# Attention and two dense layers on one core: weight conversions spread over slots 5 to 25, layer 1's last piece behind attention's last product, kept PSUM banks, and two last output transfers

## The chip, the core and the metric

One Trainium2 chip, of which the kernel uses one core. The metric is the device time of one execution in microseconds (us). The engines named below are TensorE (PE, with its weight loads as PEld), VectorE (DVE), ScalarE (ACT), GpSimd (POOL) and SyncE (SP), which here issues nearly every DMA.

## The reference, cut to what matters

Block-causal attention for 4 batches, 8 heads, 576 positions and head size 64, then two dense layers over all 2304 tokens (512 to 2048 to 512), the first with a leaky gate, the second with an exponential one.

```python
scores = scale * np.matmul(q, k.transpose(0, 1, 3, 2))
scores = np.where(block_i >= block_j, scores, -1e9)     # blocks of 64 positions
attn = softmax(scores)                                  # float32
x = np.matmul(attn, v)                                  # -> 2304 x 512
h = x @ w_in;  g = np.maximum(h, 0.0) + alpha * np.minimum(h, 0.0)
x = g @ w_out                                           # layer 1
h = x @ w2_in; g = np.where(h > 0.0, h, np.exp(np.minimum(h, 0.0)) - 1.0)
out = g @ w2_out                                        # layer 2
```

The weights arrive as 64-bit numbers. The kernel turns each into a high and a low 32-bit part, and most products are made in three passes over such parts.

## The kernel before

**Two stages.** The first is attention, as 71 *slots* (k = 0 to 70) written out by hand in `slot`; the second is both dense layers, as a list of steps behind it. Every engine executes its instructions in the order in which the program emits them. The tokens lie in five units: 0 to 3 have 512 tokens each, and unit 4 has 256, the last 64 positions of every batch (the "tails").

**Slots.** Slots 0 to 7 and 32 to 39 make the scores of the first 256 positions of a pair of heads, slots 8 to 31 and 40 to 63 those of the rest, three slots for a pair; slots 64 to 70 finish. In a slot PE makes scores (L290, L297, L302), the products of an earlier pair with v (L444) and transposes of an earlier slot's exponentials (L377, L384, L390); DVE takes maxima (L319), sums (L353, L355), low parts of x (L89) and copies of transposes (L95); ACT makes the exponentials (L346) and copies; POOL normalises (L96) and makes low parts. The product of the last pair (L444 in slot 70) gives the last piece of `x1[3]` and of the tails, which DVE finishes with two low parts (L89, outputs x and xtail).

**Weights.** `load_w` handles half of one of 16 weight tiles per layer. The DMA (L123) is issued at a slot in `w_slots`, `arrival[0]` ticks later ACT makes two conversions (L133, L134) and DVE three operations behind them (L138, L139, L143), here called the *begin*; then POOL adds (L148), ACT casts (L162) and DVE makes the low part (L89, output w), the *end*. A tick is one slot, or two pieces of layer 1. Sixteen halves are loaded beside attention: the first eight serve hidden tiles 0 to 3, the other eight hidden tiles 4 to 7.

**Layer 1 beside attention.** Three units (0, 2 and 1) go partly through layer 1 beside attention, in `l1_beside`, with the first 4 of 16 hidden tiles. Each is cut into 16 *pieces* of 6 products of 512 columns: 8 for the hidden tiles (L599) and 8 for the outputs (L611). `stretches` says from which slot to which the pieces are spread. For unit 0 the hidden pieces stand from slot 14 to 26 and the output pieces from 26 to 39: ahead of slots 26, 28, 29, 31, 33, 34, 36 and 37. The last 8 pieces of unit 1 stand one ahead of each of slots 63 to 70.

**Banks.** In attention PSUM is four banks for scores (`twin`) and banks 4 to 7, used in turn for transposes, products and layer 1's pieces (`ring("t", ...)`). Behind attention `att.close()` gives up all eight, and a new pool takes them; the dense stage uses banks 5, 6, 7 for hidden tiles (`ring("h", ...)`) and 0 to 4 for sums (`ring("acc", ...)`). Its first step is unit 3 (hidden tiles L580, outputs L684), straight from `x1[3]` in SBUF; unit 4 is next and is read back from scratch (`load_x1`, L542).

**Scratch.** Units are dumped to scratch from SP, two ticks behind the product that completes them: L424 for a unit, L426 for the tails.

**The end.** The last unit of layer 2 is unit 4, with two blocks of 128 tokens. Each block's last sum is copied from PSUM to SBUF (DVE for block 0, ACT for block 1), and then L670 writes it in two transfers of 64 rows of 2 KB. Whole blocks of other units go out at L666, one transfer of 128 rows each.

Of the kernel before, what the change touches and what calls it, by code (L numbers as in the profile page):

```python
# [9 lines left out]
F32 = mybir.dt.float32  # L10
# [6 lines left out]
PSUM = bass.MemoryType.PSUM  # L17
DRAM = bass.MemoryType.DRAM

P = 128  # L20
B, H, S, D = 4, 8, 576, 64
# [15 lines left out]
def f32(ap):  # L37
    return ap.bitcast(F32)
# [3 lines left out]
def attention_moe_kernel(ctx: ExitStack, tc: tile.TileContext, qT, kT, v_a, v_b, w1, w2, alpha, out):  # L42
    nc = tc.nc
    pe, act, dve, pool_e = nc.tensor, nc.scalar, nc.vector, nc.gpsimd
# [21 lines left out]
    rings = {}  # L66

    def ring(name, *banks):
        rings[name] = list(banks)
# [33 lines left out]
    def later(ticks, emit):  # L103
        due.setdefault(tick[0] + ticks, []).append(emit)
# [83 lines left out]


    att = ExitStack()  # L190
    ps = att.enter_context(pool("ps", 1, space=PSUM))
    twin = [ps.tile([P, 2, 512], F32, name=f"pair{i}") for i in range(2)]
    bank = [None] * 4 + [ps.tile([P, 512], F32, name=f"bank{i}") for i in range(4, 8)]
    ap1 = att.enter_context(pool("att1", 1))
    ap2 = att.enter_context(pool("att2", 2))
    vraws = [ap1.tile([P, 2, 5, D], F32, name=f"vraw{i}") for i in range(2)]
# [222 lines left out]
    def x_out(n, half):  # L419

        b, p = PAIRS[n]
        u = unit_of(n, half)
        if n % (2 * NPAIR) == 2 * NPAIR - 1:
            later(2, lambda: nc.sync.dma_start(out=xd[u], in_=f32(x1[u])))  # L424
        if half == 1:
            later(2, lambda: nc.sync.dma_start(out=xd[B][:, :, p, 64 * b:64 * b + 64], in_=f32(st[n]["tail"])))  # L426

# [227 lines left out]
    def l2_y(u, f, gs):  # L655
        for tg in range(UNITS[u] // P):
            acc = acc_bank(tg, f == 0)
            for t, (wp_, gp_) in enumerate(PASSES):
                pe.matmul(acc, gs[:, gp_, tg * P:(tg + 1) * P], w_out(1, f, wp_, 0, DM),  # L659
                          start=f == 0 and t == 0, stop=f == NF - 1 and t == 2)  # L660
            if f == NF - 1:
                o = z_tile(tg)
                copy("va"[tg % 2], o, acc)
                if u < B:
                    r = S * (2 * (u % 2) + tg // 2) + 256 * (u // 2) + P * (tg % 2)
                    nc.sync.dma_start(out=out[r:r + P, :], in_=o)  # L666
                else:
                    for k in range(2):
                        r = S * (2 * tg + k) + 512
                        nc.sync.dma_start(out=out[r:r + 64, :], in_=o[64 * k:64 * k + 64, :])  # L670


    zs = {}
# [24 lines left out]
    with tc.manual_schedule(engines={ET.PE, ET.Activation, ET.DVE, ET.Pool, ET.SP}):  # L698
        ring("s", 0, 1)
        ring("t", 4, 5, 6, 7)  # L700

        halves = [(0, f, r) for r in range(2) for f in range(FA)]
        load_early(0)
        load_early(1)
        keep_busy(6)
        for half in range(2):
            scale_early(0, slice(256 * half, 256 * half + 256), "v")
        load_early_v(0)
        load_alpha()
        for emit in other_at[-1]:  # L710
            emit()
        load_early_v(1)
        end_tick()
        LEAD = 14
        stretches = [(0, LEAD, 26, 26, X_DONE[2]), (2, X_DONE[2], 47, 47, 55), (1, 55, 63, 63, LAST)]
        w_slots = {5, 8, 10, 12, 14, 16, 18, 20}
        w_slots |= {27 + 5 * i for i in range(8)}
        halves += [(0, FA + f, r) for r in range(2) for f in range(4)]

        def slots(lo, hi):  # L720
            for k in range(lo, hi):
                if k in w_slots:
                    arrival[0] = 4 if k > 21 else 3 if k < 8 else 2
                    load_w(*halves.pop(0))
                slot(k)

        slots(0, LEAD)

        k = LEAD
        for u, a, b, c, d in stretches:  # L730
            assert a >= X_DONE[u]
            parts = l1_beside(u)
            for first, end, n in ((a, b, 2 * FA), (c, d, 2 * KC)):
                slots(k, first)
                k = first
                for j in range(n):
                    next(parts)
                    to = first + (2 * (j + 1) * (end - first) + n) // (2 * n)
                    slots(k, to)
                    k = to  # L740
        arrival[0] = 2
        assert not held and not halves and not amid
        in_slots[0] = False


    with tc.manual_schedule(engines={ET.PE, ET.Activation, ET.DVE, ET.Pool, ET.SP}):


        att.close()
        ps = ctx.enter_context(pool("ps_all", 1, space=PSUM))  # L750
        bank[:] = [ps.tile([P, 512], F32, name=f"bank{i}") for i in range(8)]
        w_pools.append(ctx.enter_context(pool("w2", NF - 8)))
        late_pools.append(ctx.enter_context(pool("late", 1)))
        ring("h", 5, 6, 7)
        ring("acc", *range(5))
        units = [("A", 3), ("A", 4)] + [("B", u) for u in (2, 0, 1)] + [
            ("D", u) for u in (4, 3)] + [("C", u) for u in (2, 0, 1, 3, 4)]
        fs = CHUNKS
        steps = [(k, u, f) for k, u in units for f in fs[k]]
        first_of = {}  # L760
        for i, (k, u, f) in enumerate(steps):
            first_of.setdefault((k, u), i)
        lag = 3
        words = sorted((3 * r + f, f, r) for f in range(8) for r in range(2))
        w_at = dict(zip((0, 1, 2, 3, 4, 5, 9, 11, 13, 17, 18, 20, 21, 22, 24, 25), ((0, 8 + f, r) for _, f, r in words)))
        w_at.update(zip((29, 31, 33, 35, 37, 41, 43, 45, 47, 48, 49, 53, 55, 57, 61, 62),
                        ((1, f, r) for f in range(8) for r in range(2))))
        w_at.update(zip((*range(64, 69), *range(71, 82)), ((1, 8 + f, r) for _, f, r in words)))
        gs = {}
        for i in range(len(steps) + lag):  # L770
            if i in w_at:
                arrival[0] = 6 if i < 6 else 4 if i < first_of["C", 2] - 4 else 2
                load_w(*w_at[i])
            if i < len(steps):
                k, u, f = steps[i]
                if f == fs[k][1]:
                    n = units.index((k, u)) + 1
                    if n < len(units) and units[n] != ("D", u):
                        (load_x2 if units[n][0] == "C" else load_x1)(units[n][1])
                gs[i] = l2_h(u, f) if k == "C" else l1_gate(f, l1_h(u, f), UNITS[u])  # L780
            end_tick()
            if i >= lag:
                k, u, f = steps[i - lag]
                if k == "C":
                    l2_y(u, f, gs.pop(i - lag))
                else:
                    l1_y(k, u, f, gs.pop(i - lag))
            end_tick()
# [32 lines left out]
```

## Time and profile before

| what | value |
|---|---|
| runs | 984.2, 984.25, 985.19 us (median 984.25) |
| the profiled execution, own time | 985.47 us |
| its span, first to last instruction | 983.7 us |
| PE busy | 959.4 us (98%) |
| DVE, ACT, POOL busy | 549.5, 438.4, 341.6 us |
| mean granted TensorE clock | 0.996 of full speed |

The profiled execution takes 985.47 us, 1.7 us more than its span, which is launch and end around the instructions; it stands 1.2 us above the median. PE is nearly always busy, so that what is left to look at are the short stretches in which it isn't, and the time behind its last product.

### The profile page before, as it was taken

The page shows a single profiled execution, that of the slowest core. Times are in us where ns is not written, and L with a number is a line of the kernel's source. Part 1 is how long each engine was busy: PE and PEld are TensorE (multiplying, and loading weights), DVE is VectorE, ACT ScalarE, POOL GpSimd, SP SyncE. Part 2 cuts the span into 40 slices and gives each one's busy share as a digit, 9 for nine tenths or more (in the row PEclk, how much of TensorE's full clock was granted, in tenths as well). Part 3 has the DMA queues.
Part 4 walks back from the last instruction along what each step waited for, and adds up shares of the span by engine and source line. Part 5 has one row for each costly group of instructions (what it writes and reads, how often), then busy time and mean ns, then how long its engine had stood idle before and what let it go on. Part 6 is the DMA issues. An engine that isn't in the chain of part 4 may idle for free.

```text
span 983.7 us, 13873 instructions
## 1 busy us (share of the span) xinstructions
PE 959.4 (98%) x5064; PEld 779.2 (79%) x5064; DVE 549.5 (56%) x1012; ACT 438.4 (45%) x985; POOL 341.6 (35%) x401
## 2 busy tenths in 40 slices
PE   9888999999999999999999999999999999999997
PEld 7556666776789888888888888888888888888896
DVE  6999777775375454543554685994333332433343
ACT  6877787675354443433433553652222222222232
POOL 6888678664264343433443551330000000000000
PEclk9999999999999999999999999999999999999999
DMA  6553574432545522612537444322002100200010
GB/s 197 197 162 95 149 239 161 136 90 94 199 141 175 184 80 85 214 32 97 170 109 244 162 151 150 107 84 109 1 1 86 44 1 0 86 1 1 1 43 22
DMA packets 55524, 105.77 MB, mean 108 GB/s; under 512 B 11040, under 2 KB 29472, under 8 KB 54304
## 3 DMA queue, kind: packets, MB, share of 16 engines
q1 hardware_dynamic: 55168, 104.62, 32.2%
q8 instruction: 40, 0.66, 0.3%
q14 instruction: 28, 0.23, 0.1%
q10 hardware_dynamic: 288, 0.26, 0.1%
HBM read 76.55 MB, written 28.31 MB: 107 GB/s over the span
## 4 chain that ended last, share of the span: by engine, by line
PE 89%; DVE 5%; issue 2%; ACT 2%; POOL 1%; DMA 1%; SPq 0%; POOLq 0%; ACTq 0%; DVEq 0%
PE bank L634 20%; PE bank L659 20%; PE bank L580 16%; PE bank L684 16%; PE bank L444 4%; PE bank L611 3%; PE bank L599 2%; PE bank L384 2%; PE pair L297 1%; PE pair L290 1%; PE bank L377 1%; PE bank L207 1%; PE pair L302 1%; DVE wword L143 1%; DMA wraw<-w 1%
## 5 line engine op out<-in xcount | busy, mean ns | idle before, releaser
L634 PE MATMUL bank<-x,w 128*128 128x512 f32 (+1 forms) x960 | 210.0, 368 | 0.0
L634 PEld LDWEIGHTS bank<-x,w 128*128 128x128 f32 x960 | 169.4, 188 | 31.1
L580 PE MATMUL bank<-x,w 128*128 128x512 f32 (+1 forms) x816 | 175.5, 365 | 3.1 <-DVE g L560 1.9
L580 PEld LDWEIGHTS bank<-x,w 128*128 128x128 f32 x816 | 141.3, 189 | 27.9 <-DVE g L560 2.1
L560 DVE SCALAR_TENSOR_TENSOR g<-neg,beta,bank 128x512 f32<-128x512 f32 (+1 forms) x80 | 55.3, 692 | 130.5 <-ACT neg L557 130.4
L639 DVE TENSOR_SCALAR e<-e 128x512 f32<-128x512 f32 (+1 forms) x80 | 33.6, 420 | 165.5 <-ACT e L638 165.5
L148 POOL TENSOR_TENSOR wword<-wword,wraw 128x512 int32<-128x512 int32 x64 | 92.7, 1448 | 80.8 <-DVE wword L143 60.9
L638 ACT ACTIVATE e<-bank 128x512 f32<-128x512 f32 (+1 forms) x80 | 44.2, 552 | 168.5 <-PE bank L634 168.5
L659 PE MATMUL bank<-w,gs 128*128 128x512 f32 x432 | 104.7, 390 | 0.0
L659 PE MATMUL bank<-w,gsl 128*128 128x512 f32 x432 | 104.7, 390 | 0.0
L96 POOL TENSOR_SCALAR p<-p,stat 128x256 f32<-128x256 f32 (+4 forms) x144 | 85.0, 605 | 31.1 <-DVE stat L355 17.2
L659 PEld LDWEIGHTS bank<-w,gs 128*128 128x128 f32 x432 | 80.6, 188 | 16.3
L659 PEld LDWEIGHTS bank<-w,gsl 128*128 128x128 f32 x432 | 80.6, 188 | 16.3
L557 ACT ACTIVATE neg<-bank 128x512 f32<-128x512 f32 (+1 forms) x80 | 44.0, 550 | 102.6 <-PE bank L580 102.2
L89 POOL TENSOR_TENSOR gs<-g,gs 128x512 fp32r<-128x512 f32 (+1 forms) x46 | 56.5, 1229 | 94.8 <-ACT gs L564 94.8
L346 ACT ACTIVATE p<-pair,stat 128x256 f32<-128x256 f32 (+4 forms) x144 | 77.9, 551 | 24.5 <-DVE stat L319 18.9
L684 PE MATMUL bank<-gs,w 128*128 128x512 f32 (+1 forms) x408 | 87.8, 365 | 0.0
L684 PE MATMUL bank<-gsl,w 128*128 128x512 f32 (+1 forms) x408 | 87.8, 365 | 0.0
L684 PEld LDWEIGHTS bank<-gs,w 128*128 128x128 f32 x408 | 70.7, 189 | 12.2
L684 PEld LDWEIGHTS bank<-gsl,w 128*128 128x128 f32 x408 | 70.7, 189 | 12.2
L143 DVE SCALAR_TENSOR_TENSOR wword<-wraw,wword 128x512 uint32<-128x512 uint32 x64 | 74.3, 1161 | 2.2
L89 DVE TENSOR_TENSOR w<-wword,w 128x512 fp32r<-128x512 f32 x64 | 65.4, 1021 | 15.6 <-ACT w L162 15.4
(82 smaller groups left out, 1249.4 us busy)
## 6 DMA issues: line engine op xcount, KB each, us to landing
wraw<-w SPq DMA_DIRECT2D x64, 512.0 KB, 4.7
xd<-x SPq DMA_DIRECT2D x4, 2048.0 KB, 7.5
x<-xd SPq DMA_DIRECT2D x16, 512.0 KB, 7.0
x<-yd SPq DMA_DIRECT2D x4, 2048.0 KB, 9.5
vraw<-v_a SPq DMA_DIRECT2D x24, 256.0 KB, 3.6
kraw<-kT SPq DMA_DIRECT2D x16, 288.0 KB, 4.5
yd<-gs SPq DMA_DIRECT2D x8, 512.0 KB, 3.4
yd<-gsl SPq DMA_DIRECT2D x8, 512.0 KB, 3.1
```

What stands on the lines that cost most here:

```text
L89: return {"v": dve, "p": pool_e}[eng].tensor_tensor(out=out, in0=x, in1=f32(high), op=ALU.subtract)
L96: return pool_e.tensor_scalar(out, x, 1.0 if scale is None else scale, 1.0, ALU.mult, ALU.mult)
L143: dve.scalar_tensor_tensor(out=wi, in0=high, scalar=0xC0000000, in1=wi, op0=ALU.bitwise_and, op1=ALU.bitwise_or)
L148: pool_e.tensor_tensor(out=w, in0=w, in1=units, op=ALU.add)
L346: act.activation(out=out, in_=x, func=AF.Exp, bias=stat[:, k:k + 1], accum_out=stat[:, SUMS + 2 * k:SUMS + 2 * k + 1])
L557: act.activation(out=neg, in_=h, func=AF.Relu, scale=-1.0)
L560: dve.scalar_tensor_tensor(out=g, in0=neg, scalar=beta[:, f:f + 1], in1=h, op0=ALU.mult, op1=ALU.add)
L580: pe.matmul(h, w_in(0, f, wp_, kc), x[:, xp_, kc, :n], start=kc == 0 and t == 0, stop=kc == KC - 1 and t == 2)
L634: pe.matmul(h, w_in(1, f, wp_, kc), x[:, xp_, kc, :], start=kc == 0 and t == 0, stop=kc == KC - 1 and t == 2)
L638: act.activation(out=e, in_=h, func=AF.Exp)
L659: pe.matmul(acc, gs[:, gp_, tg * P:(tg + 1) * P], w_out(1, f, wp_, 0, DM), start=f == 0 and t == 0, stop=f == NF - 1 and t == 2)
L684: pe.matmul(acc, w_out(0, f, wp_, m * P, P), gs[:, gp_, :n], start=first and t == 0, stop=last and t == 2)
```

## The change

- `w_slots`: the first eight weight halves are loaded at slots 5, 9, 12, 15, 18, 21, 23, 25 (before 5, 8, 10, 12, 14, 16, 18, 20), the other eight at 30, 35, 39, 44, 49, 54, 58, 63 (before 27, 32, ... 62). `arrival[0]` becomes 4 behind slot 26, not behind slot 21.
- The output pieces of unit 0 are spread from slot 32 to 39: ahead of slots 32, 33, 34, 35, 36 (two), 37, 38.
- In the last stretch the piece before the last keeps its place, and the last one (6 products) stands behind slot 70.
- Banks 4 to 7 lie in a pool that stays; the dense stage takes the three banks of the attention ring that were used longest ago for hidden tiles, and the fourth as fifth bank for sums.
- The dump of unit 3 is emitted 8 ticks behind its product, not 2; the tails' dump stays at 2 and so comes first.
- The last block's copy is split between ACT and DVE, 256 columns each, and each block goes out in one transfer whose destination is 2 times 64 rows, instead of two transfers of 64 rows.

```diff
     att = ExitStack()
+    ps = ctx.enter_context(pool("ps_kept", 1, space=PSUM))
+    bank = [None] * 4 + [ps.tile([P, 512], F32, name=f"bank{i}") for i in range(4, 8)]
     ps = att.enter_context(pool("ps", 1, space=PSUM))
     twin = [ps.tile([P, 2, 512], F32, name=f"pair{i}") for i in range(2)]
-    bank = [None] * 4 + [ps.tile([P, 512], F32, name=f"bank{i}") for i in range(4, 8)]
...
-            later(2, lambda: nc.sync.dma_start(out=xd[u], in_=f32(x1[u])))
+            later(8 if u == B - 1 else 2, lambda t=x1[u]: nc.sync.dma_start(out=xd[u], in_=f32(t)))
...
-                copy("va"[tg % 2], o, acc)
+                if u == B and tg == 1:
+                    act.copy(o[:, :256], acc[:, :256])
+                    dve.tensor_copy(o[:, 256:], acc[:, 256:])
+                else:
+                    copy("va"[tg % 2], o, acc)
...
-                    for k in range(2):
-                        r = S * (2 * tg + k) + 512
-                        nc.sync.dma_start(out=out[r:r + 64, :], in_=o[64 * k:64 * k + 64, :])
+                    rows = out.rearrange("(b s) c -> b s c", s=S)
+                    nc.sync.dma_start(out=rows[2 * tg:2 * tg + 2, 512:, :], in_=o)
...
-        stretches = [(0, LEAD, 26, 26, X_DONE[2]), (2, X_DONE[2], 47, 47, 55), (1, 55, 63, 63, LAST)]
-        w_slots = {5, 8, 10, 12, 14, 16, 18, 20}
-        w_slots |= {27 + 5 * i for i in range(8)}
+        stretches = [(0, LEAD, 26, 32, X_DONE[2]), (2, X_DONE[2], 47, 47, 55), (1, 55, 63, 63, LAST)]
+        w_slots = {5, 9, 12, 15, 18, 21, 23, 25}
+        w_slots |= {30, 35, 39, 44, 49, 54, 58, 63}
...
-                    arrival[0] = 4 if k > 21 else 3 if k < 8 else 2
+                    arrival[0] = 4 if k > 26 else 3 if k < 8 else 2
...
+                    if end == LAST and j == n - 2:
+                        to = LAST
...
-        bank[:] = [ps.tile([P, 512], F32, name=f"bank{i}") for i in range(8)]
+        bank[:4] = [ps.tile([P, 512], F32, name=f"bank{i}") for i in range(4)]
...
-        ring("h", 5, 6, 7)
-        ring("acc", *range(5))
+        oldest = rings["t"]
+        ring("h", *oldest[:3])
+        ring("acc", *range(4), oldest[3])
```

## Rows read from the trace of the kernel before

**Rows 1.** Busy time per engine over the span, from the page's first part

```profile
PE 959.4 (98%) x5064; PEld 779.2 (79%) x5064; DVE 549.5 (56%) x1012; ACT 438.4 (45%) x985; POOL 341.6 (35%) x401
```

**Rows 2.** Stretches: length; PE, PEld, DVE, ACT, POOL busy (instructions); clock; DMA share, GB/s

```profile
24.16:92.17 68.01, 55.93 (x364) 39.39 (x363) 64.74 (x137) 51.62 (x137) 58.19 (x75) 0.95 0.49 155
92.17:110.94 18.77, 18.53 (x134) 13.43 (x133) 14.08 (x35) 14.02 (x39) 13.79 (x22) 1.00 0.43 129
110.94:140.71 29.77, 29.77 (x220) 19.94 (x220) 23.38 (x69) 22.27 (x84) 20.83 (x40) 1.00 0.66 208
140.71:252.14 111.43, 109.43 (x723) 78.80 (x722) 75.20 (x183) 72.88 (x189) 69.56 (x97) 1.00 0.39 127
```

**Rows 3.** Timeline of PE: start, us, instruction [idle before, releaser]; two longest stalls

```profile
54.06 2.62 PE L599 MATMUL bank<-x,w 128*128 128x512 f32 x6 [2.25 <-DVE pt L95]
...
76.57 0.63 PE L390 MATMUL bank<-ident,p 128*128 128x128 f32 x4 [3.20 <-DVE xtail L89]
```

**Rows 4.** DVE's groups by shape, 24.16 to 92.17: count, busy us, mean ns, idle before

```profile
L89 DVE TENSOR_TENSOR w<-wword,w 128x512 fp32r<-128x512 f32 x7 | 8.2, 1178 | 0.0
L143 DVE SCALAR_TENSOR_TENSOR wword<-wraw,wword 128x512 uint32<-128x512 uint32 x8 | 7.7, 968 | 0.3
...
L139 DVE TENSOR_SCALAR wword<-wword 128x512 uint32<-128x512 uint32 x8 | 4.8, 599 | 0.3
...
L138 DVE TENSOR_SCALAR wword<-wword 128x512 f32<-128x512 f32 x8 | 4.6, 574 | 0.4 <-ACT wword L133 0.4
```

**Rows 5.** The same view, 92.17 to 110.94

```profile
L89 DVE TENSOR_TENSOR w<-wword,w 128x512 fp32r<-128x512 f32 x1 | 0.7, 693 | 0.6 <-ACT w L162 0.6
L143 DVE SCALAR_TENSOR_TENSOR wword<-wraw,wword 128x512 uint32<-128x512 uint32 x1 | 0.7, 693 | 0.0
```

**Rows 6.** Timeline around slot 46

```profile
164.17 0.69 DVE L143 SCALAR_TENSOR_TENSOR wword<-wraw,wword 128x512 uint32<-128x512 uint32 x1
...
167.34 1.66 PE L611 MATMUL bank<-gs,w 128*128 128x512 f32 x6 [1.22 <-DVE x L89]
```

**Rows 7.** Timeline around slots 62 and 63

```profile
228.35 0.63 ACT L162 CAST w<-wword 128x512 fp32r<-128x512 f32 x1
...
232.24 0.73 PE L611 MATMUL bank<-gs,w 128*128 128x512 f32 x2 [0.52 <-POOL gs L89]
```

**Rows 8.** Timeline from slot 68 into the dense stage

```profile
246.79 3.00 PE L611 MATMUL bank<-gs,w 128*128 128x512 f32 x12
247.05 0.59 ACT L93 COPY pt<-bank 128x512 f32<-128x512 f32 x1
...
249.72 2.42 PE L444 MATMUL bank<-pt,vraw 128*64 128x320 f32 x20
...
253.05 0.21 DVE L89 TENSOR_TENSOR xtail<-bank,xtail 128x64 fp32r<-128x64 f32 x1
...
253.41 4.82 PE L580 MATMUL bank<-x,w 128*128 128x512 f32 x20 [1.27 <-DVE xtail L89]
```

**Rows 9.** Timelines of SP and PE: unit 4's loads and first product

```profile
255.63 5.69 SPq L542 DMA_DIRECT2D x<-xd  x4
...
288.90 1.59 PE L580 MATMUL bank<-x,w 128*128 128x256 f32 x12
```

**Rows 10.** Timeline behind the last product

```profile
978.40 0.58 ACT L93 COPY zl<-bank 128x512 f32<-128x512 f32 x1 [3.79 <-PE bank L659]
978.45 1.18 SPq L670 DMA_DIRECT2D out<-z  x2
```

**Rows 11.** DMA view of 977 to 984: packets, bytes and packet sizes

```profile
DMA packets 320, 0.52 MB, mean 75 GB/s; under 512 B 64, under 2 KB 64, under 8 KB 320
```

**Rows 12.** SP's issue of L666 (timeline), and two stretches as in rows 2

```profile
937.68 0.33 SPq L666 DMA_DIRECT2D out<-z  x1
...
938.52:941.25 2.73, 2.73 (x20) 2.48 (x19) 1.15 (x3) 0.79 (x2) 0.00 (x0) 1.00 1.00 383
979.65:982.33 2.68, 0.00 (x0) 0.00 (x0) 0.00 (x0) 0.00 (x0) 0.00 (x0) 1.00 0.85 195
```

## The prediction

> **What bounds the kernel now.** Read the page's busy time first: PE works in 959.4 us of 983.7 [rows 1], so everything that the change can win is among some 24 us. The table by stretch then says where PE waits [rows 2]. The four stretches are slots 8 to 25, 26 to 31, 32 to 39, and 40 to the last product. In the first PE is busy for 55.9 of 68.0 us, at a granted clock of 0.95, and DVE for 64.7 (95%). In the second PE has 18.5 of 18.8 us, in the third all of 29.8, in the fourth 109.4 of 111.4. So slots 8 to 25 hold 12.1 us of PE's idle time, and DVE is their bound. PE's two longest stalls there end on DVE, behind which they queue [rows 3]. DVE's groups show the reason: eight begins and seven ends of weight halves in these 68 us, a begin at 0.574 + 0.599 + 0.968 = 2.14 us, an end at 1.18 us, against 0.69 us for an end where POOL is less dense [rows 4, 5]. Last the two seams: 1.27 us between attention's last product and the dense stage [rows 8], and the time behind the last product, which begins at about 978.4 us [rows 10].
>
> **Weights, slots 8 to 25.** Counting ticks (a slot is one, two pieces of layer 1 are one), begins fall in slots 8, 11, 14, 16, 19, 22, 25, 27, not 8, 10, 12, 14, 16, 18, 19, 22; ends in 11, 14, 16, 19, 22, 25, 28, 30, not 11 to 25. Seven begins and six ends remain there. One begin and one end less is 2.14 + 1.18 = 3.3 us of DVE [rows 4]; at DVE's present 95% that is -3.5 us. The bounds are 0 (DVE finds other waits) and -13.5 us (PE alone, 55.9 less one piece).
>
> **Layer 1's four moved pieces.** A piece costs about 1.4 us: twelve products issue in 246.79 to 249.72, which is two pieces [rows 8]. The pieces ahead of slots 26, 28, 29 and 31 go behind slot 31. Slots 26 to 31 lose three and get one (ahead of 32): PE 18.5 - 2.8 = 15.7 us. DVE's work there stays at about 14.1: one more end comes, one copy of a sum goes, and one begin stands for another [rows 2]. With DVE at 14.1 beside PE at 15.7 I take 16.8, so -2.0 us (bounds -2.8, and 0 if their waits on each other keep 18.8). Slots 32 to 39 get three more pieces on a PE that is busy in all of its 29.8 us: +4.2 us, with nothing to hide them [rows 2]. So the three stretches give -3.5 - 2.0 + 4.2 = -1.3 us. What is won in the first is mostly paid in the third.
>
> **Weights, slots 40 to 63.** The begin at slot 45 goes to 47. It now stands ahead of slot 46's maxima on DVE until 164.86, and a piece waits 1.22 us for the low part at the end of that queue [rows 6]; without it I take -0.6. The cast of the 15th half goes from slot 62 to 63: 0.63 us of ACT ahead of the gate of the last hidden tile, for which PE waits 0.52 us [rows 7], so -0.4. New waits may come where the work lands (0 to +1 us in all). Together -1.0, bounds 0 and -2.
>
> **Last piece and banks.** Of the two pieces in 246.79 to 249.72 one goes behind the product. The product then starts at about 248.2, and its transposes are copied by 247.05 + 0.59 = 247.64 [rows 8], so 0.5 us of cover is left. The moved piece, 1.4 us, lies over ACT's casts and DVE's low parts (1.27 us until PE starts [rows 8]). The dense stage needs `x1[3]`, whose low part comes just ahead of the tails', and a bank; with the banks kept it takes the two whose transposes were copied at 247.64, with no wait for the tails' low part. Both together: -1.27 us (bounds -1.3 and -0.2: if the bank wait stayed, only a little of the cover would count).
>
> **Dumps.** On SP the dump of unit 3 goes behind the tails' dump, one weight load, unit 4's four loads and one more weight load. Those loads are out by 261.3, and unit 4's first product is at 288.90 [rows 9]: 27 us hide it, so nothing either way. The loads that overwrite unit 3's buffer wait until unit 3 is through, also then, well behind an unhurried dump. If that cover were gone, unit 4 would wait for its loads.
>
> **The last outputs.** Before, each of four transfers takes SP 0.59 us to issue, from 978.45 [rows 10], and the traffic ends at 982.33 [rows 12]. The four have 320 packets, 256 of them rows of 2 KB and 64 small ones, 16 per transfer [rows 11]: each runs on all 16 engines. After, each of two transfers has 128 rows, but its destination is a pattern of 2 by 64 rows, which can't be one run, because 512 other rows lie between its halves. Every transfer of the program before has at least 64 as its outer dimension. None shows one of 2, so I bound it. **End (a):** the rows spread over 16 engines as now. The whole-block transfers of the unit before move 383 GB/s with the engines always busy [rows 12], 23.9 GB/s for one engine, 85.6 ns for a row of 2 KB. Traffic starts 0.84 us behind the issue (937.68 to 938.52 [rows 12]). The second issue comes at about 979.05, so the end is 979.05 + 0.84 + 8 x 0.0856 = 980.6: -1.7 us. **End (b):** the transfer is cut by its outer dimension, one half per engine, and both transfers use the same two engines. Then one engine has 128 rows: 128 x 0.0856 = 10.95 us from 978.45 + 0.84 = 979.29, the end is 990.2, and that is +7.9 us. At the pace of the tails' own rows (195 GB/s, 168 ns a row [rows 12]) it would be 21.5 us and +18.5; the rows of whole blocks are nearer, being 128 rows at once like the new ones. I take (b): the division over the outer dimension fits each transfer that the trace has, as does (a), but only (b) has a reason to be different for a 2. The copy split between ACT and DVE (0.58 us whole [rows 10]) is worth nothing in (a), where SP is still issuing the first transfer, and nothing in (b).
>
> The Trainium skill, "DMA: Bandwidth & Descriptors", section "Why a DMA increments its semaphore by 16 and not by 1", speaks against this edit: the generator looks at the slowest dimension of either pattern that isn't 1, and takes the largest number of engines up to 16 that divides both. For 128 and 2 that is two engines, and the sum is (b)'s; were the rule not to hold as stated, it is (a)'s. By that rule all transfers of the trace would have 16, as the 64 small packets show for the last four [rows 11]; no row shows fewer.
>
> **Sum.** On the profiled span: -1.3 - 1.0 - 1.27 + 7.9 = +4.3, 983.7 to 988.0; its execution takes 985.47 and the median is 984.25, so I add the difference to the median: **988.6 us**.
>
> **Rivals.**
> 1. The last rows spread over 16 engines, end (a): 984.25 - 3.57 - 1.7 = 979.0, faster. For it: 16 engines in each of the transfers shown [rows 11], and that a 128-row source is there to be divided. Against it: the 2 by 64 pattern. The point from which it decides: five engines or more (256 rows x 85.6 ns / 5 = 4.4 us, ends 983.7, +1.4).
> 2. Two engines, but with fewer begins and ends in slots 8 to 25 each of them falls to the price of the quieter stretch: six ends from 1.18 to 0.69 us and the last operation of seven begins from 0.97 to 0.69 us are another 2.9 + 1.9 = 4.8 us of DVE [rows 4, 5], which PE can use there, having 12.1 us idle: 988.6 - 4.8 = 983.8, no change. Against it: POOL, beside which they are dear, stays busy for most of the stretch (58.2 of 68.0 us now [rows 2]).
> 3. Two engines, and the emptied slots 26 to 31 don't get shorter, because score, maximum, exponential and the next score wait on each other: 0 for -2.0; the idle time that opens on PE lowers its granted clock, as in 24.16 to 92.17 (0.95 over 68 us is 3.4 us of lost clock [rows 2]), and half of that, 1.7 us, falls on slots 32 to 39, where PE has no slack: 988.6 + 2.0 + 1.7 = 992.3.
> 4. The banks kept don't remove the wait for the tails' low part, and only the rest comes true: 988.6 + 1.1 = 989.7.
>
> **How the numbers follow.** The forecast has 0.50, rival 1 0.25, rival 2 0.10, rival 3 0.10, rival 4 0.05. Around the forecast alone the attention terms can miss by 2.5 us either way: 986 to 991. The range must reach into rival 1 and rival 3: 978.0 to 992.5, which leaves out a part of rival 1 and what lies above rival 3, end (b) at the slow pace among it. A measurement of this kernel tells 0.2%, 2 us, from no change. Faster: rival 1 nearly whole and a little of rival 2, 0.26. Same: the most of rival 2 and the edges of the others, 0.11. Slower: 0.63.
>
> **What would show it.** Last outputs: over the end of the trace the DMA view has few small packets (2 per transfer, 4 in all, not 32) at about 48 GB/s for 11 us if (b) holds, 32 small packets and an end near 980 us if (a) does. Weights: over slots 8 to 25 PE's idle time falls by about 2 us net and the stretch to 64.5 us; slots 26 to 31 take about 16.8 and 32 to 39 about 34.0. Seam: L580 follows L611 with no idle time, and the last piece stands behind the last L444. Slot 46's stall falls to about 0.6, slot 63's to nearly none. The prediction is wrong if the last traffic is short, or if slots 8 to 25 shrink by more than 6 us.

## The result and the profile after

The changed kernel takes 993.77 us (median of 5 runs, 992.68 to 995.2) where the kernel before takes 984.2 (983.64 to 985.19) beside it: a ratio of 1.0094, 95% interval 1.0083 to 1.0106. It is 9.6 us slower. The forecast was 988.6, so the direction and the reason for most of it were right, and the time lies 1.3 us above the range.

The profiled execution of the changed kernel takes 994.62 us with a span of 992.8, against 985.47 and 983.7 before: 9.1 us of span, nearly the whole difference. The tables below split it by stretch, with the bounds of [rows 2] moved to the same slots. The first part of the page says that PE does as much as before (961.2 us beside 959.4 in [rows 1]) in a longer span:

```profile
PE 961.2 (97%) x5064; PEld 780.0 (79%) x5064; DVE 551.4 (56%) x1013; ACT 438.1 (44%) x985; POOL 343.2 (35%) x401
```

The table by stretch of the changed kernel, columns as in [rows 2] (slots 8 to 25, 26 to 31, 32 to 39, 40 to about the end of the last product):

```profile
24.11:86.63 62.52, 54.38 (x357) 38.45 (x357) 57.53 (x127) 47.77 (x130) 52.71 (x72) 0.95 0.50 161
86.63:107.31 20.68, 17.93 (x121) 12.45 (x121) 18.70 (x43) 16.32 (x44) 19.70 (x25) 0.92 0.59 167
107.31:141.16 33.85, 33.85 (x236) 23.06 (x236) 23.67 (x68) 23.25 (x84) 18.57 (x37) 1.00 0.52 160
141.16:252.60 111.44, 108.35 (x718) 77.73 (x718) 77.19 (x186) 73.28 (x192) 73.33 (x100) 1.00 0.42 139
```

The first row is 5.5 us shorter than before, the second 1.9 longer although it holds one piece where it held three, the third 4.1 longer. DVE shows what happened: it lost 7.2 us in the first row (64.74 to 57.53) and got 4.6 in the second (14.08 to 18.70), where POOL also rose from 13.79 to 19.70. The last row is as long as before, though one piece (1.4 us) has moved behind the product.

The tail, in the timeline of the changed kernel (start, us, instruction, and in brackets the idle time before it with its releaser); these lines answer to [rows 10]:

```profile
977.94 0.69 DVE L95 COPY z<-bank 128x512 f32<-128x512 f32 x1 [2.66 <-PE bank L660]
978.62 0.37 ACT L665 COPY zl<-bank 128x256 f32<-128x256 f32 x1 [3.79 <-PE bank L660]
978.66 0.66 SPq L674 DMA_DIRECT2D out<-z  x1
979.02 0.42 DVE L666 COPY zl<-bank 128x256 f32<-128x256 f32 x1 [0.39 <-ACT zl L665]
979.48 0.54 SPq L674 DMA_DIRECT2D out<-zl  x1
```

PE ends at 978.58, 0.2 us later than before (978.37). From there to the end of the span it was 5.38 us and is 14.26. Three stretches of 2 us of this tail, and the DMA view of 977 to 993 (GB/s in 40 equal slices, then packets):

```profile
979.90:981.90 2.00, 0.00 (x0) 0.00 (x0) 0.00 (x0) 0.00 (x0) 0.00 (x0) 1.00 0.13 28
981.90:983.90 2.00, 0.00 (x0) 0.00 (x0) 0.00 (x0) 0.00 (x0) 0.00 (x0) 0.62 0.13 38
983.90:985.90 2.00, 0.00 (x0) 0.00 (x0) 0.00 (x0) 0.00 (x0) 0.00 (x0) 0.50 0.13 51
```

```profile
GB/s 0 0 0 0 0 20 0 31 10 31 41 15 36 41 36 15 51 51 51 51 51 51 51 51 51 51 51 51 51 51 51 51 51 51 51 51 31 0 0 0
DMA packets 261, 0.53 MB, mean 33 GB/s; under 512 B 4, under 2 KB 4, under 8 KB 260
```

Look at three numbers. There are 4 small packets, 2 for each transfer, where [rows 11] has 16 for each. The DMA share is 0.13 throughout, which is 2 of 16 engines always busy and 14 idle (2 / 16 = 0.125). And the rate settles at 51 GB/s, where whole blocks move 383 and the old tails 195 [rows 12]. So the last 512 KB take from 979.93 to 991.67.

The sum of the prediction beside the profiles, in us:

| term | forecast | profile of after |
|---|---|---|
| slots 8 to 25 | -3.5 | -5.5 |
| slots 26 to 31 | -2.0 | +1.9 |
| slots 32 to 39 | +4.2 | +4.1 |
| slots 40 to 63 and on, without the seam | -1.0 | +1.3 |
| seam | -1.27 | -1.2 |
| start of the dense stage to PE's end (not forecast) | 0 | -0.3 |
| PE's end to the end of the span | +7.9 | +8.9 |
| sum | +4.3 | +9.2 |

The fourth line is 111.3 us (141.16 to the product's end at 252.49) less 111.43 before, with the piece of 1.4 us that left counted back. The sum, 9.2, stands for 9.1 us of span. Two terms have the wrong sign, slots 26 to 31 and slots 40 to 63: together they are 6.2 us off. Slots 8 to 25 gave 2.0 more than was forecast, the tail cost 1.0 more.

### The profile page after: what moved, and what is told of

It is laid out like the page before. It is cut to its first block, busy times and chain, and to the rows that moved or that the text cites. A ratio compares the mean times of both kernels' runs of the same rounds, so it can differ in the third digit from the quotient of the medians.

```text
span 992.8 us, 13864 instructions
## 1 busy us (share of the span) xinstructions
PE 961.2 (97%) x5064; PEld 780.0 (79%) x5064; DVE 551.4 (56%) x1013; ACT 438.1 (44%) x985; POOL 343.2 (35%) x401
## 4 chain that ended last, share of the span: by engine, by line
PE 85%; DVE 4%; POOL 4%; ACT 3%; issue 2%; DMA 1%; SPq 0%; ACTq 0%; POOLq 0%; DVEq 0%
PE bank L635 20%; PE bank L660 20%; PE bank L581 16%; PE bank L688 16%; PE bank L612 3%; PE bank L445 3%; PE bank L600 2%; PE pair L291 1%; PE bank L385 1%; ACT p L347 1%; POOL p L96 1%; PE pair L298 1%; PE bank L208 1%; PE bank L378 1%; POOL wword L148 1%
## 5 line engine op out<-in xcount | busy, mean ns | idle before, releaser
L635 PEld LDWEIGHTS bank<-x,w 128*128 128x128 f32 x960 | 169.3, 188 | 31.2
L581 PE MATMUL bank<-x,w 128*128 128x512 f32 (+1 forms) x816 | 175.3, 364 | 1.7 <-DVE g L561 1.7
L581 PEld LDWEIGHTS bank<-x,w 128*128 128x128 f32 x816 | 141.3, 189 | 26.4 <-DVE g L561 1.9
L96 POOL TENSOR_SCALAR p<-p,stat 128x256 f32<-128x256 f32 (+4 forms) x144 | 87.7, 623 | 33.5 <-DVE stat L356 20.9
```

The source lines that it names most:

```text
L96: return pool_e.tensor_scalar(out, x, 1.0 if scale is None else scale, 1.0, ALU.mult, ALU.mult)
L581: pe.matmul(h, w_in(0, f, wp_, kc), x[:, xp_, kc, :n], start=kc == 0 and t == 0, stop=kc == KC - 1 and t == 2)
L635: pe.matmul(h, w_in(1, f, wp_, kc), x[:, xp_, kc, :], start=kc == 0 and t == 0, stop=kc == KC - 1 and t == 2)
```

## The experiments

Each run stands beside runs of the kernel before on the same chip, whose median was 984.2 to 984.3 in each group. A difference in us is between medians.

### The outputs

**Only the new outputs on the kernel before.**

```diff
-                copy("va"[tg % 2], o, acc)
+                if u == B and tg == 1:
+                    act.copy(o[:, :256], acc[:, :256])
+                    dve.tensor_copy(o[:, 256:], acc[:, 256:])
...
-                    for k in range(2):
-                        r = S * (2 * tg + k) + 512
-                        nc.sync.dma_start(out=out[r:r + 64, :], in_=o[64 * k:64 * k + 64, :])
+                    rows = out.rearrange("(b s) c -> b s c", s=S)
+                    nc.sync.dma_start(out=rows[2 * tg:2 * tg + 2, 512:, :], in_=o)
```

> The kernel before with the new last outputs alone (split copy, one transfer of 2 by 64 rows per block). Theory A (each of these transfers runs on two engines, and that is the whole of the loss): the product stages stay as before, PE ends at about 978.4, the DMA view of the end has 4 small packets at about 50 GB/s, traffic ends about 9 us later than before, time 984.2 + 8.9 = 993.1 (992 to 994.5). Rival B (the outputs cost about 4 us, the rest is lost in attention or by the slower clock): 988.

Measured: 993.16 us (992.64 to 994.58), ratio 1.0092 (1.0076 to 1.0107), +8.9. PE ends at 978.55 and the tail is 14.25 us, as in the changed kernel. The DMA view of its last 35 us has the same 4 small packets:

```profile
DMA packets 262, 0.55 MB, mean 16 GB/s; under 512 B 4, under 2 KB 4, under 8 KB 260
```

So 8.9 of the 9.6 us come from these lines alone, whatever stands before them.

**The changed kernel, but each last transfer to one run of rows.** The split copy and the two issues stay; only the destination is 128 rows in one run, so that the second half of each block lands on other rows than the reference's.

```diff
-                    rows = out.rearrange("(b s) c -> b s c", s=S)
-                    nc.sync.dma_start(out=rows[2 * tg:2 * tg + 2, 512:, :], in_=o)
+                    r = 2 * S * tg + 512
+                    nc.sync.dma_start(out=out[r:r + P, :], in_=o)
```

> The changed kernel, but each last transfer writes its 128 rows as one run of 128 rows. The rows land partly in another batch's place: this leaves out the right placing of the last 64 rows of each odd batch. Number of transfers, bytes and source are the changed kernel's; only the destination's pattern differs. If the pattern's outer dimension of 2 is the cause: 32 small packets, rows of 2 KB on 16 engines, traffic over within about 1.7 us of the second issue, time 993.8 - 10.5 = 983.3 (982 to 984.5). If the cause is that two transfers are fewer than four, or the late second issue: it stays near 993.

Measured: 982.45 us (982.22 to 984.81), ratio 0.9985 (0.9976 to 0.9994). The tail's timeline, its DMA packets (960 to 985), and a stretch of its traffic:

```profile
976.92 0.33 SPq L674 DMA_DIRECT2D out<-z  x1
...
977.74 0.33 SPq L674 DMA_DIRECT2D out<-zl  x1
```

```profile
DMA packets 290, 0.55 MB, mean 22 GB/s; under 512 B 32, under 2 KB 32, under 8 KB 288
```

```profile
978.50:979.30 0.80, 0.00 (x0) 0.00 (x0) 0.00 (x0) 0.00 (x0) 0.00 (x0) 1.00 0.86 333
```

The same number of issues and the same bytes now have 32 small packets, 16 for each transfer, a DMA share of 0.86 and 333 GB/s. The tail is 3.82 us, 1.56 shorter than before. That is end (a) of the prediction, which said -1.7. So neither the number of transfers nor the split copy costs the 8.9 us; the destination of 2 by 64 rows does.

**The changed kernel with the four old transfers and the whole copy.**

> The changed kernel with the last outputs as before (four transfers of 64 rows, whole copy); all else changed. Theory A: 993.8 - 8.9 = 984.9 (984 to 986), no change against before, because what the seam gives (1.3) is lost again in slots 26 to 63. My forecast's terms for attention and seam (-3.6) would give 980.6. Rival B: about 989.

Measured: 985.25 us (983.57 to 988.0), ratio 1.0015 (1.0004 to 1.0026). The tail is back at 5.59 us. What remains of the change is worth about +0.9 us, where the prediction's other terms gave -3.6. The run with one run of rows lies 2.8 us lower with a tail that is 1.8 us shorter, so that by it the rest would be nearer to nothing; either way it is far from -3.6. This run separates the tail, which was understood, from attention, which was not.

### The seam

**Only the kept banks, the last piece and the later dump on the kernel before.**

> The kernel before with the kept banks, the last piece behind attention's last product, and the later dump alone. Forecast's term: the 1.27 us ahead of the dense stage's first product goes, nothing else moves, 984.2 - 1.3 = 982.9. Rival: PE waits elsewhere for what the shorter cover leaves (transposes' copies, sums' banks), 984.2.

Measured: 982.78 us (982.08 to 983.97), ratio 0.9986 (0.9978 to 0.9995), -1.5 by the medians. The changed kernel's own seam, in its timeline, answers to [rows 8]:

```profile
250.07 2.42 PE L445 MATMUL bank<-pt,vraw 128*64 128x320 f32 x20
252.43 1.65 PE L612 MATMUL bank<-gs,w 128*128 128x512 f32 x6
253.40 0.21 DVE L89 TENSOR_TENSOR xtail<-bank,xtail 128x64 fp32r<-128x64 f32 x1
253.92 8.32 PE L581 MATMUL bank<-x,w 128*128 128x512 f32 x36
```

The last piece (L612) follows the product with no idle time, covers the tails' low part at 253.40, and the dense stage (L581) follows with none. The forecast of -1.27 us holds.

**Only the last piece is moved; the new pool takes all eight banks as before.**

```diff
                     to = first + (2 * (j + 1) * (end - first) + n) // (2 * n)
+                    if end == LAST and j == n - 2:
+                        to = LAST
```

> The kernel before with only the last piece of six products behind attention's last product; banks and dumps as before. If the piece's 1.4 us by itself cover the wait for the tails' low part (which ends 1.1 us behind the last product), the seam's idle time goes without kept banks: 984.2 - 1.3 = 982.9. If the new pool's banks wait for something later, a part of the 1.27 us stays: 983.5 to 984.2.

Measured: 984.37 us (983.36 to 985.82), ratio 0.9999 (0.999 to 1.0007): no gain. Its seam:

```profile
252.62 1.65 PE L611 MATMUL bank<-gs,w 128*128 128x512 f32 x6
...
254.31 0.69 DVE L95 COPY z<-bank 128x512 f32<-128x512 f32 x1 [0.50 <-PE bank L611]
...
255.15 7.07 PE L580 MATMUL bank<-x,w 128*128 128x512 f32 x30 [0.88 <-DVE z L95]
```

The piece hides the tails' low part, but now PE waits 0.88 us for the copy of the piece's own result. The dense stage's banks come here from a new pool, and its first product starts only behind that copy, the last reader of an old bank. So the moved piece alone gives nothing, and with the kept banks and the later dump it gives 1.3 to 1.5 us; what the kept banks give alone no run shows. Rival 4 of the prediction (the banks kept don't help) falls.

**The seam, and block 1's two transfers issued from ACT.** The edit on top of the seam's is one line: `(nc.scalar if tg else nc.sync).dma_start(...)`.

> The kernel before with the seam (kept banks, last piece, later dump), and the last block's two transfers of 64 rows issued from ACT, not from SP. The last two issues then start at once behind ACT's copy (979.05) and not at 979.7: -0.6 against the seam alone, 982.8 - 0.6 = 982.2. Rival: issues of two queues share the descriptor generation and nothing is won, 982.8.

Measured: 983.29 us (981.8 to 984.45), ratio 0.9983 (0.9972 to 0.9994). In the profiles the tail is 4.92 us instead of 5.37, but the medians, 983.29 here and 982.78 for the seam alone, don't show it, and the expected 982.2 didn't come. A second queue is worth at most some 0.4 us here, and these runs can't tell it from nothing.

### The weights and the pieces

**Only the weights' slots and the pieces' place on the kernel before** (`w_slots`, `arrival[0]` and `stretches` as in the change).

> The kernel before with the new weight slots, the new limit for the longer arrival, and unit 0's output pieces from slot 32, and nothing else. Theory A, from the changed kernel's trace: slots 8 to 25 win 5.5 us, slots 26 to 31 lose 1.9, slots 32 to 39 lose 4.1, later stalls (slots 46, 47, 58, 63) lose 1.2: 984.3 + 1.7 = 986.0 (985 to 987). My forecast's terms (-1.3 and -1.0) give 982.0.

Measured: 986.67 us (985.7 to 988.28), ratio 1.0024 (1.0015 to 1.0033), +2.5. The prediction had -2.3 for this part. With the outputs alone (+8.86) and the seam alone (-1.52) the three parts add up to 9.8, so the change (9.6) is about the sum of its parts. In this profile slots 26 to 31 took 21.99 us, and 6.83 us of them ran at half the clock:

```profile
86.79:108.78 21.99, 19.25 (x120) 12.51 (x121) 19.21 (x44) 16.86 (x45) 19.99 (x26) 0.84 0.57 162
...
95.80:102.63 6.83, 6.07 (x28) 3.25 (x26) 6.20 (x15) 3.85 (x11) 6.82 (x8) 0.50 0.86 239
```

**The same, with the later eight halves at their old slots** (27, 32, ... 62).

> As the one with the weight slots alone, but the later eight halves keep their slots (27, 32, ... 62). If the longer stalls from slot 46 on come from the later eight halves' new slots, slots 40 to the last product take 111.4 us again and the time is 984.3 + 0.5 = 984.8; also slots 26 to 31 get one more begin from slot 30 on. Rival: the stalls there come from elsewhere, time stays at 986.

Measured: 984.99 us (983.9 to 986.78), ratio 1.0005 (0.9996 to 1.0013). Slots 26 to 31, and slots 40 to 62:

```profile
86.49:107.43 20.94, 18.05 (x121) 12.55 (x121) 18.97 (x44) 16.60 (x45) 19.95 (x25) 0.92 0.60 163
...
141.31:229.78 88.47, 86.97 (x578) 62.75 (x578) 65.43 (x158) 63.60 (x168) 62.89 (x88) 1.00 0.41 132
```

The first eight and the pieces are worth +0.8, so the later eight's new slots cost the other 1.7. The profiles say where most of it lies: slots 40 to 62 take 88.47 us here and 88.46 before, but 89.30 in the changed kernel, whose stalls of PE over slots 46 to 63 are these:

```profile
164.98 0.87 PE L445 MATMUL bank<-pt,vraw 128*64 128x256 f32 x8 [0.22 <-DVE x L89]
...
167.88 1.67 PE L612 MATMUL bank<-gs,w 128*128 128x512 f32 x6 [1.00 <-DVE x L89]
172.55 0.73 PE L612 MATMUL bank<-gs,w 128*128 128x512 f32 x2 [0.48 <-POOL gs L89]
214.68 1.66 PE L600 MATMUL bank<-x,w 128*128 128x512 f32 x6 [0.54 <-DVE xtail L89]
233.95 0.73 PE L612 MATMUL bank<-gs,w 128*128 128x512 f32 x2 [0.85 <-POOL gs L89]
```

Slot 46's wait of 1.22 us [rows 6] became two, 0.22 and 1.00. The last one, in slot 63, rose from 0.52 to 0.85 [rows 7], the one at 172.55 is new, and the one at 214.68 was 0.15. Together they are 3.09 us where before they were 1.89. In this run, with the old slots, they are 1.23, 0.15 and 0.53 again. So the stalls hold 1.2 of the 1.7 us; the rest is within the spread of the runs.

**The weights' slots as in the change, the pieces from slot 30.** Theory A was that slots 26 to 31 are bound by DVE and POOL with PE free, so that pieces put back there cost nothing.

> As the one with the weight slots alone, but unit 0's output pieces are spread from slot 30, not from 32: ahead of slots 30, 31, 32, 33, 35, 36, 37, 38. Two pieces more then lie in slots 26 to 31. Theory A: that stretch is bound by DVE (18.7 of 20.7 us busy in the changed kernel), so that two pieces are free there: slots 32 to 39 take 31.1 us, not 33.9, and the time is 986.0 - 2.7 = 983.3. Rival: PE with its halved clock or the chain of scores bounds it, pieces cost what they cost: 986.

Measured: 986.57 us (985.72 to 988.89), ratio 1.0024 (1.0015 to 1.0033). The expected gain isn't there. Slots 26 to 31 and 32 to 39:

```profile
86.41:109.90 23.49, 19.48 (x132) 13.17 (x132) 19.91 (x46) 17.98 (x47) 21.04 (x27) 1.00 0.48 144
109.90:141.33 31.43, 31.17 (x225) 20.88 (x224) 23.00 (x64) 21.62 (x80) 17.55 (x35) 1.00 0.53 173
```

Two pieces more cost 2.6 to 2.8 us in the first row (23.49 beside 20.68 in the changed kernel and 20.85 in the one with the four old transfers) and save 2.4 in the second. PE's timeline of this run says why they aren't free. Its idle time lies ahead of them, in slots 27 to 29: 1.37 us for DVE, then 0.60 and 1.25 for POOL, the last until 97.26. The two pieces come at 101.19 and 104.15, and the second waits another 0.38 and 0.41 us for its own weights, whose end comes this late by the new slots. The row also has a clock of 1.00, so the half clock of the runs above isn't what makes these slots long: slot 29's score starts 10.85 us behind the start of the row here (97.26) and in the changed kernel (97.48), where 3.4 us at half the clock begin at 94.93. There PE is slower and then waits 0.18 us for POOL instead of 1.25.

**Only the pieces' place: unit 0's output pieces from slot 32 on the kernel before.**

> The kernel before with unit 0's output pieces from slot 32 and nothing else: slots 26 to 31 are emptied, but get no more weight work than before. Theory C (in the changed kernel these slots are long because two begins and three ends of weight halves and their POOL adds land there): slots 26 to 31 take about 16.0 us here (PE's own work), slots 32 to 39 33.9, time 984.2 + 1.3 = 985.5. Rival 3 of the prediction (emptied slots don't get shorter, as score, maximum, exponential and next score wait on each other, and the granted clock falls to half there): 18.8 to 20.7 us there, time 988 to 990.

Measured: 987.23 us (985.97 to 987.84), ratio 1.0028 (1.0017 to 1.0039), +2.9. Slots 26 to 31 and 32 to 39:

```profile
91.39:108.61 17.22, 16.23 (x122) 11.16 (x121) 14.72 (x37) 13.41 (x39) 15.51 (x23) 1.00 0.62 165
108.61:142.47 33.86, 33.86 (x237) 23.05 (x236) 23.88 (x68) 23.35 (x86) 20.95 (x40) 1.00 0.52 177
```

With one piece instead of three and with the old weights' slots, slots 26 to 31 do get shorter: 18.77 to 17.22, with PE at 16.23 and DVE at 14.72. The forecast's 16.8 was worked out from nearly these two numbers. But the run has less weight work there than the forecast: one end and no begin, since a piece that moves also moves the ticks, and with them the begin of the ninth half from slot 30 to slot 31, where it comes behind that slot's own work and so outside the row. So rival 3's chain of score, maximum and exponential isn't the reason that these slots got longer in the changed kernel. Beside the run with the later eight at their old slots (20.94 us) this one differs only in the first eight's slots and their delay, so the weight work that these bring there, two begins and two ends more, is worth about the 3.7 us between the two (the clock of that row was 0.92, which by the run above costs little there). The run also shows what the move costs: 1.6 us won, 4.1 lost. The expectation of 985.5 us was 1.7 too low.

### A version faster than both

**The seam, and the first eight spread less.** On top of the seam's edit:

```diff
-        stretches = [(0, LEAD, 26, 26, X_DONE[2]), (2, X_DONE[2], 47, 47, 55), (1, 55, 63, 63, LAST)]
-        w_slots = {5, 8, 10, 12, 14, 16, 18, 20}
+        stretches = [(0, LEAD, 26, 27, X_DONE[2]), (2, X_DONE[2], 47, 47, 55), (1, 55, 63, 63, LAST)]
+        w_slots = {5, 8, 11, 13, 16, 18, 20, 22}
...
-                    arrival[0] = 4 if k > 21 else 3 if k < 8 else 2
+                    arrival[0] = 4 if k > 22 else 3 if k < 8 else 2
```

> The seam alone (982.8) with a smaller spread: the first eight halves at slots 5, 8, 11, 13, 16, 18, 20, 22, unit 0's output pieces from slot 27, the later eight halves as before. All but the last end then fall by slot 25. If the loss in slots 26 to 31 comes from begins and ends that land there, slots 8 to 25 win some 3 us, slots 26 to 31 take about 20 with four pieces, slots 32 to 39 29.8 as before: 982.8 - 1.8 = 981.0. Rival: what the spread wins is lost again one for one, 982.8.

Measured: 980.0 us (978.46 to 983.92), ratio 0.996 (0.9945 to 0.9974): 4.3 us faster than the kernel before and 2.8 faster than the seam alone (which ran on another chip); 981.0 was expected. Slots 8 to 25, 26 to 31 and 32 to 39:

```profile
23.78:85.71 61.93, 51.44 (x357) 36.18 (x357) 59.17 (x130) 50.11 (x135) 55.98 (x73) 1.00 0.51 166
85.71:107.22 21.51, 20.29 (x139) 14.27 (x139) 18.46 (x44) 15.52 (x42) 17.13 (x23) 1.00 0.50 140
107.22:137.04 29.82, 29.78 (x218) 19.83 (x218) 23.33 (x67) 22.08 (x84) 21.09 (x40) 1.00 0.63 200
```

The three sum to 113.26 us, where it was 116.55 before and 117.05 in the changed kernel. The first row keeps the gain of the wider spacing; the third stays at 29.8 us because it holds four pieces, as before. The fourth piece of the second row, ahead of slot 32, is one that stood in the first. In the profiled run the clock was full in all three rows (0.95 in the first row of [rows 2]), which is part of the gain: PE's 357 instructions are busy for 51.44 us here and 54.38 in the changed kernel. How much of the median's gain is the clock and how much the spacing these runs don't tell exactly. The run with a mean clock of 0.995 took 980.05 us, 0.9 and 1.6 more than the two at 0.998, and no run of the seam alone (0.994 to 0.997) was below 982.08, so that most of the 2.8 us is likely the spacing.

## Why the prediction was right or wrong

**The outputs: the mechanism right, the term 1 us short.** Of the two ends the prediction took (b), two engines and +7.9. The 4 small packets, the share of 0.13 and the first experiment (+8.9) say so; rival 1 falls, and the run with one run of rows gives end (a) as soon as the 2 is gone. What the term missed can be read in the tail. The first packet came 1.27 us behind the issue (978.66 to 979.93), not 0.84: +0.43. For 4 us the two engines moved only 28 and 38 GB/s, 132 KB where 51 GB/s would be 204 KB: 72 / 51 = +1.4. Then a row took 2 x 2048 B / 51 GB/s = 80 ns, not 85.6: 128 rows are 0.7 shorter. That is +1.2 from the issue to the last packet; the span ends 1.17 us behind that packet and not 1.42 as before, which leaves +1.0. The run with the outputs alone begins as slowly (29 and 37 GB/s); why, no run here tells. The slow pace, 168 ns a row and +18.5, which the prediction put aside, didn't come.

The Trainium skill, "DMA: Bandwidth & Descriptors", section "Why a DMA increments its semaphore by 16 and not by 1", says that the largest number of engines up to 16 that divides the slowest dimension of both patterns is taken. The trace agrees: 2 small packets for each transfer with a 2 there, 16 with a 128. The section adds that on the hardware queues it is the lowest-numbered engines. No view here names an engine; the trace agrees as far as the share of 0.13 while both transfers are under way says that both use the same two.

**Copy split: worth nothing, as forecast, and for one more reason.** DVE's half waits 0.39 us for ACT's half of the same tile (979.02 behind 978.62), so the two halves run one behind the other and end at 979.44, where the whole copy's 0.58 us from 978.62 would end at 979.20.

**Slots 8 to 25 and 26 to 31: the step that failed is the count of weight work by slot.** The prediction counted a begin in the slot in which ACT's two conversions are emitted. But DVE's three operations come due one tick later, at that slot's end and behind its own work, in `load_w`:

```python
            first()
            later(1, bits)
            later(1, sign)
```

An end counted in slot 25 is emitted behind that slot's own work too, which DVE reaches when PE is in slot 26. The rows had the sign of it: counted by slot, eight ends fall in slots 8 to 25 before, where [rows 4] has seven and [rows 5] the eighth. So not one begin and one end left slots 8 to 25, but two of each (eight and seven in [rows 4], six and five after), which is why that stretch won 5.5 instead of 3.5 us. They came down in slots 26 to 31, where the prediction had one begin and two ends. DVE's timeline of the changed kernel has two begins (the last operation of each stands for it) and three ends, where [rows 5] has one of each, and PE's has waits that are new:

```profile
88.82 0.69 DVE L89 TENSOR_TENSOR w<-wword,w 128x512 fp32r<-128x512 f32 x1 [0.56 <-ACT w L162]
...
91.01 0.69 DVE L143 SCALAR_TENSOR_TENSOR wword<-wraw,wword 128x512 uint32<-128x512 uint32 x1
...
97.70 1.06 DVE L143 SCALAR_TENSOR_TENSOR wword<-wraw,wword 128x512 uint32<-128x512 uint32 x1
...
100.60 0.73 DVE L89 TENSOR_TENSOR w<-wword,w 128x512 fp32r<-128x512 f32 x1 [0.45 <-ACT w L162]
...
105.65 1.12 DVE L89 TENSOR_TENSOR w<-wword,w 128x512 fp32r<-128x512 f32 x1
```

```profile
93.66 0.30 PE L395 MATMUL bank<-ident,p 128*64 128x128 f32 x1 [1.38 <-DVE xtail L89]
94.56 0.38 PE L303 MATMUL pair<-kh,qdiag 128*128 128x288 f32 x1 [0.59 <-POOL kh L96]
...
97.48 0.69 PE L298 MATMUL pair<-kh,qh 64*128 64x384 f32 x2 [0.18 <-POOL p L96]
...
104.19 0.38 PE L303 MATMUL pair<-kh,qdiag 128*128 128x288 f32 x1 [0.55 <-POOL wword L148]
```

At 93.66 PE waits 1.38 us for a low part that stands on DVE behind the begin that ends at 91.70 and the maxima of a slot; that begin is the one that the prediction had in slot 25. DVE is at 18.70 of 20.68 us and POOL at 19.70, so 16.8 could not be held. With that work elsewhere 17.22 came out. PE waits first for DVE, then three times for POOL; which of the two binds these slots no run separates. So the stretch that gave up pieces got weight work in their place, and the pieces cost their full price, +4.1, where PE has no slack; that term was right. Rival 2's cheaper operations hardly came: in slots 8 to 25 an end cost 1.02 us instead of 1.18, a begin 2.15 as before.

**Slots 40 to 63: two gains named, neither came.** The prediction took -0.6 at slot 46 and -0.4 at slot 63 because a begin and a cast move away from there. At slot 46 nothing was won: its waits, 0.22 and 1.00 us, add up to the old 1.22. The begin is gone from there, but an end took its place, that of the half loaded at slot 39. ACT's cast for it, at 161.72, waits 2.20 us for POOL's add, and DVE's low part behind it, at 162.37, 1.86 us for the cast, so that DVE comes to the low part of x no earlier. The prediction moved the begins by slot and didn't ask what the ends would stand ahead of. Three other waits grew by 1.2 us together. "New waits may come where the work lands" was in the text with 0 to +1 us and then went into the sum at nearly zero. With the later eight at their old slots, 1.7 us of the median come back, 0.8 us of slots 40 to 62 and 0.3 us of slot 63's wait among them.

**Seam: right, by its own steps,** and the run with the last piece alone shows that "if the bank wait stayed" was the right alternative to bound: it gave nothing, near the bound of -0.2.

**The dumps: nothing, as forecast.** No wait of unit 4 for its loads shows, and the seam as a whole gives the -1.27 us. No run has the later dump alone.

**The range.** Rival 3 gave 992.3 for slots 26 to 31 that don't get shorter, by the wrong reason: it wasn't the chain of score and maximum, and slots 32 to 39 ran at a clock of 1.00. The upper end of 992.5 took each miss alone. Here three steps failed at once and all went the same way: the new place of weight work in slots 40 to 63 (+2.3 us against the forecast), the count of begins and ends in slots 8 to 39 (+1.8 net, +0.5 for the forecast's -1.3), and the size of the tail (+1.0). The +/-2.5 us that the prediction allowed for attention didn't hold the first two together. That the time still lies near the range is in part luck, since the 2.0 us that slots 8 to 25 gave beyond the forecast come from the same wrong count that lost 3.9 in slots 26 to 31.

## What to carry to other kernels

Write a transfer so that the slowest dimension of both its patterns divides by 16; one with a 2 there ran on two engines here, and at the end of a kernel nothing hides it: two transfers in place of four cost 8.9 us. When work is spread over slots, count it where the engine executes it, with each deferred step and the queue ahead of it, and list for the stretch that receives it the busy time of every engine, not only of the one that was relieved. A step that waits for another engine, as an end does, can hold up a queue longer than the begin that it replaces. Work that leaves a slot with idle time for one where the main engine is full is paid in full (+4.1 us for three pieces).

## What the runs showed of the hardware

- Two engines sum to 51 GB/s on rows of 2 KB, 80 ns a row and engine, after a first 4 us at 28 and 38 GB/s. The old tails' transfers, 64 rows at once, moved 195 GB/s with all 16 engines at a share of 0.85 [rows 12]; the same bytes in two transfers of 128 rows in one run moved 333 at 0.86. So a row took longer in the four transfers of 64 rows (16 x 2 KB x 0.85 / 195 GB/s = 143 ns of an engine) than in the two of 128 (85 ns). Whether it is the 64 partitions of the source or that the four transfers are twice as many no run separates.
- The granted clock falls to half (1.2 GHz) for stretches of 3.4 us in attention in most profiles, and where they lie differs between kernels whose order there is the same: 40.8 and 54.5 before, 62.6 and 76.3 in the run with the outputs alone, 63.2 in the seam's run with two queues, 31.2 and others with the last piece alone. Kernels that differ only behind attention can so differ by a microsecond or two in it (PE's end at 978.58, 977.30 and 976.85 in the changed kernel and its two variants with other outputs, with three, two and one such stretches). Where PE waits for another engine anyway a stretch can cost nothing: slot 29's score starts 10.85 to 10.91 us behind slot 26 in four profiles in which one lies between, and at 10.85 in the one at full clock.
- In the changed kernel the clock is at half from 982.39 on. PE has had nothing to do since 978.58, so it costs nothing, but the mean clock of the page (0.99 beside 0.996) contains it and says little of attention.
